# A decode step's attention: query projection with the row as weights, a first transfer in two, and one output block moved to the end

## The chip, the cores and the metric

The kernel runs on one core of a Trainium2 chip. The metric is the time of one execution on the device in microseconds (us). The program is told in terms of the core's engines: PE (TensorE, the matmuls, with its weight loads as PEld), DVE (VectorE), ACT (ScalarE), POOL (GpSimd) and SP (SyncE, which here issues nearly all transfers). 16 DMA engines move data between HBM and the on-chip memory SBUF; PSUM is the memory that PE writes to. SBUF and PSUM have 128 lanes (partitions).

## The reference

Four sequences decode one token each. The row x (4 x 640) is normed, goes through an attention with 32 heads over a cache of 4096 keys and values per head, and beside it through a small gated MLP; both results are added to x.

```python
def _A_ref(x, k_cache, v_cache, wq, wo):        # x (4,1,640), caches (4,32,4096,128)
    q = (x @ wq).reshape(B, Sq, Hq, Dh).transpose(0, 2, 1, 3)
    scores = jnp.einsum('bhqd,bhkd->bhqk', q, k) * Dh ** (-0.5)
    p = _softmax(scores, axis=-1)
    o = jnp.einsum('bhqk,bhkd->bhqd', p, v)
    return o.transpose(0, 2, 1, 3).reshape(B, Sq, Hq * Dh) @ wo

def _B_ref(x, w_in, w_sp, b_sp, w_out):         # w_in (640,1728), w_out (864,640)
    z = _gelu(jnp.einsum('bsd,df->bsf', x, w_in))
    z1, z2 = z[..., :Fh], _layernorm(z[..., Fh:], axis=-1)
    g = jnp.einsum('ts,bsf->btf', w_sp, z2) + b_sp[None, :, None]
    return jnp.einsum('bsf,fd->bsd', z1 * g, w_out)

xn = _layernorm(x, axis=-1)
return x + _A_ref(xn, k_cache, v_cache, wq, wo) + _B_ref(xn, w_in, w_sp, b_sp, w_out)
```

Everything is bfloat16. The two caches are 134 MB each, wq and wo 5.2 MB each; together with the MLP's weights some 282 MB are read once.

## The kernel before

**Tiles.** A tile is four heads of one sequence: 4 heads x 4096 keys x 128 values, 4 MB, laid out so that each of the 128 lanes holds 128 rows of the cache (32 KB in one piece). There are 32 K tiles and 32 V tiles, numbered i = 4 hg + b with the head group hg (0 to 7) and the sequence b (0 to 3).

**SBUF slots and the order of transfers.** Five slots of 4 MB (`KV_SLOTS`, pool `kv`) take turns. First the two parts of wq (4 MB and 1 MB, lines 90 to 93) and the MLP's weights sit in three of them, then K and V tiles in the order of the list `loads` (line 128). `pump` (line 140) issues the next load on SP when the slot's former occupant is in the set `used`. The last V tile comes in four pieces (`V_CUTS`: 64, 32, 16 and 16 of 128 columns). The output weights wo come in eight blocks of 640 KB, one a head group, into a pool of their own with one buffer (`wop`, line 69): block hg at tile i = 4 hg + 2 (line 698), the last block after the loop in four quarters (lines 155 to 157), so that it is the last thing in the queue. All these go through one hardware queue, SP's. Each transfer counts on one of eight completion semaphores in turn, so SP issues one only when the eighth before it has landed.

**The start.** x comes in on ACT's queue and is normed (lines 239 to 255); xn is turned into xnT, 128 lanes x 5 chunks x 4 sequences (lines 257 to 264). The query projection takes each of 160 blocks of wq (32 heads x 5 chunks, 128 x 128) as the matmul's weights and xnT's 4 columns as the moving part (lines 266 to 276), which gives q turned: 128 lanes x 32 heads x 4. `stage_q(i)` (line 421) makes the query of tile i ready for DVE: once a head group it transposes 16 rows back and copies them (`q_rows`), and for every tile it spreads them over 128 lanes with one matmul and one ACT copy (`qbc`). Then `gmlp` runs the MLP.

**A tile's work.** DVE multiplies K by the query in two halves (`product`, line 439) and folds 128 values to 64 (`fold_half`, line 448); PE sums them on with the identity (`sums`); DVE finishes the row sums and maxima; ACT takes the exponential; POOL lays the 128 probabilities of each lane out as matmul weights (line 517); PE multiplies them with V in four column groups of PSUM (`blocks`, line 526). After the fourth tile of a group, `group_den`, `group_norm`, `group_turn` and `group_pick` norm and turn the result, and `group_proj` (line 627) multiplies it by the wo block with 8 matmuls into the sum `out_ps`.

**The order** on PE, DVE, ACT and SP is written by hand in the loop from line 655 on, one tile behind another; POOL's is left to the scheduler. The end (lines 700 to 722): the last tiles' blocks, `pairs` for the last V pieces, `group_norm(7)`, `group_proj(7)`, two copies and two transfers out.

Of the kernel before, what the change touches and what calls it, by code (L numbers as in the profile page):

```python
# [9 lines left out]
FP32 = mybir.dt.float32  # L10
BF16 = mybir.dt.bfloat16
# [10 lines left out]
def kernel(  # L22
# [14 lines left out]
    nc = tc.nc  # L37
    P = nc.NUM_PARTITIONS
    Bsz, Sq, D = A_x.shape
    _, H, S, Dh = A_k_cache.shape  # L40
# [3 lines left out]
    DC = D // P  # L44
# [4 lines left out]
    HT = 4  # L49
    HG = H // HT  # L50
    NT = HG * Bsz
    LN = P // HT
    NC = HT * S // P
    HC = NC // 2
# [11 lines left out]
        edge = ctx.enter_context(tc.tile_pool(name="edge", bufs=1))  # L66
        edge.tile([P, skip], mybir.dt.uint8, name="edge")
    kv = ctx.enter_context(tc.tile_pool(name="kv", bufs=KV_SLOTS))
    wop = ctx.enter_context(tc.tile_pool(name="wop", bufs=1))
    const = ctx.enter_context(tc.tile_pool(name="const", bufs=1))  # L70
    work = ctx.enter_context(tc.tile_pool(name="work", bufs=1))
    small = ctx.enter_context(tc.tile_pool(name="small", bufs=2))
# [3 lines left out]
    ps_m = ctx.enter_context(tc.tile_pool(name="ps_m", bufs=2, space=PSUM))  # L76
# [11 lines left out]
    wq_v = A_wq.rearrange("(p c) n -> p c n", c=DC)  # L88
    wq_parts = []
    for c0, c1 in ((0, HT), (HT, DC)):  # L90
        t = slot("wq")[:, 0 : (c1 - c0) * HD].rearrange("p (c n) -> p c n", n=HD)
        nc.sync.dma_start(out=t, in_=wq_v[:, c0:c1, :])  # L92
        wq_parts += [(t, i) for i in range(c1 - c0)]

    wsp_bf = const.tile([1, 1], BF16)
# [9 lines left out]
        out=w_out_sb[:, 0:NFF, :], in_=B_w_out[0 : NFF * P].rearrange("(p k) n -> p k n", k=NFF)  # L105
# [47 lines left out]
    def load_wo(j):  # L153
        wo_tiles[j] = wop.tile([P, HT, D], BF16, name="wo")
        if j == HG - 1:
            for hh in range(HT):
                nc.sync.dma_start(out=wo_tiles[j][:, hh, :], in_=wo_h[j][:, hh, :])
            return
        nc.sync.dma_start(out=wo_tiles[j][:].rearrange("p r n -> p (r n)"), in_=wo_r[j])
# [5 lines left out]
    ident = const.tile([P, P], BF16)  # L165
# [9 lines left out]
    lane_diag = const.tile([P, LN], FP32)  # L175
    nc.vector.tensor_reduce(
        out=lane_diag[:],
        in_=ident_f[:].rearrange("p (h l) -> p l h", h=HT),
# [3 lines left out]
    for hh in range(HT):  # L182
        ps = slice(hh * LN, (hh + 1) * LN)
# [5 lines left out]
    CG = P // LN  # L189
# [3 lines left out]
    for e in range(2):  # L193
        nc.vector.tensor_reduce(
            out=sel[:, :, :, e],
            in_=ident_f[:].rearrange("p (g e k h) -> p e k h g", g=CG, e=2, k=GC)[:, e],
# [6 lines left out]
    for hh in range(HT):  # L203
# [3 lines left out]
        out=spread[:],  # L207
# [6 lines left out]
    q_lanes = const.tile([HT * Bsz, Bsz, P], BF16)  # L214
    nc.vector.tensor_copy(
        out=q_lanes[:].rearrange("r b (h l) -> r b h l", h=HT),
        in_=ident[: HT * Bsz, : HT * Bsz]
        .rearrange("r (h b) -> r b h", b=Bsz)[:, :, :, None]
        .to_broadcast([HT * Bsz, Bsz, HT, LN]),
    )  # L220

    hmask_bf = const.tile([P, HT], BF16)
    nc.vector.tensor_copy(out=hmask_bf[:], in_=hmask[:])

# [34 lines left out]
    for c in range(DC):  # L259
        nc.tensor.transpose(  # L260
            out=xnT_ps[:, c, :], in_=xn_v[:, c, :], identity=ident[:Bsz, :Bsz]
        )
    xnT = const.tile([P, DC, Bsz], BF16)
    nc.vector.tensor_copy(out=xnT[:], in_=xnT_ps[:])

    q_ps = ps_m.tile([P, H, Bsz], FP32, tag="m", name="q_ps")
    for h in range(H):
        for c in range(DC):
            t, i = wq_parts[c]
            nc.tensor.matmul(  # L270
                out=q_ps[:, h, :],
                lhsT=t[:, i, h * Dh : (h + 1) * Dh],
                rhs=xnT[:, c, :],
                start=(c == 0),
                stop=(c == DC - 1),
            )
    qT = const.tile([P, H, Bsz], BF16)
    nc.vector.tensor_copy(out=qT[:], in_=q_ps[:])  # L278

# [26 lines left out]
    def gmlp():  # L308
        zz, gw, gt, gz, sq = (gm[n] for n in ("zz", "gw", "gt", "gz", "sq"))
        zT = ps_pv.tile([P, 2, NFC, Bsz], FP32, tag="pv", name="zT")  # L310
        for t in range(2):
            f1 = t * Fh + NFF * P
            w_t = w_in_sb[:, :, t * Fh : f1].rearrange("p c (f k) -> p c k f", k=NFF)
            for k in range(NFC):
                for c in range(DC):
                    nc.tensor.matmul(
                        out=zT[: P if k < NFF else FT, t, k, :],
                        lhsT=w_t[:, c, k, :] if k < NFF else w_in_sb[:, c, f1 : f1 + FT],
                        rhs=xnT[:, c, :],
                        start=(c == 0),  # L320
                        stop=(c == DC - 1),
                    )
# [93 lines left out]
    qbcs, scores, pvs, blocks_sb = {}, {}, {}, {}  # L416
    sums_ps, maxes = {}, {}

    q_rows = {}

    def stage_q(i):
        hg, b = divmod(i, Bsz)
        if b == 0:
            qr_ps = ps_m.tile([HT * Bsz, Dh], BF16, tag="m", name="qr_ps")
            nc.tensor.transpose(
                out=qr_ps[:],
                in_=qT[:, HT * hg : HT * (hg + 1), :].rearrange("p h b -> p (h b)"),
                identity=ident[:],
            )
            q_rows[hg] = small.tile([HT * Bsz, Dh], BF16, name="q_rows")  # L430
            nc.scalar.copy(out=q_rows[hg][:], in_=qr_ps[:])  # L431
        qb_ps = ps_m.tile([P, Dh], FP32, tag="m", name="qbc_ps")
        nc.tensor.matmul(  # L433
            out=qb_ps[:], lhsT=q_lanes[:, b, :], rhs=q_rows[hg][:], start=True, stop=True
        )
        qbcs[i] = small.tile([P, Dh], BF16, name="qbc", bufs=3)
        nc.scalar.copy(out=qbcs[i][:], in_=qb_ps[:])  # L437

    def product(i, half):
        t = k_tiles[i][:, half * HC : (half + 1) * HC, :]  # L440
        nc.vector.tensor_tensor(  # L441
            out=t,
            in0=t,
            in1=qbcs[i][:, None, :].to_broadcast([P, HC, Dh]),
            op=ALU.mult,
        )

# [141 lines left out]
    def group_norm(hg):  # L589
        o_n = small.tile([P, HT, Bsz], BF16, name="o_n")  # L590
        nc.vector.tensor_tensor(
            out=o_n[:], in0=pvs.pop(hg)[:], in1=gr[hg][:], op=ALU.mult
        )
        gr[hg] = o_n
# [32 lines left out]
    def group_proj(hg):  # L627
        o_n = gr.pop(hg)
        for hh in range(HT):
            for half in range(2):  # L630
                nc.tensor.matmul(  # L631
                    out=out_sum(half),
                    lhsT=o_n[:, hh, :],
                    rhs=wo_tiles[hg][:, hh, half * NOH : (half + 1) * NOH],
                    start=False,
                    stop=(hg == HG - 1 and hh == HT - 1),
                )

    def group(i, fn):
        if 0 <= i < NT and i % Bsz == Bsz - 1:  # L640
            fn(i // Bsz)
# [13 lines left out]
    E = mybir.EngineType  # L655
    with tc.manual_schedule(engines={E.PE, E.DVE, E.Activation, E.SP}):
        stage_q(0)
        stage_q(1)
        gmlp()
        used.update(occupants[:3])  # L660
        pump()
        for i in range(NT):
            j = turns.get(i)
            product(i, 0)
            at(i - 1, row_sums, 1)
            at(i - 1, lane_max)
            at(i - 1, lay_max)
            at(i - 1, spread_max)
            group(turns.get(i - 1, -1), group_pick)
            group(turns.get(i - 1, -1), group_proj)  # L670
            fold_half(i, 0)
            at(i - 1, head_max)
            at(i - 1, exps)
            sums(i, 0)
            product(i, 1)
            if i + 2 < NT:
                stage_q(i + 2)
            due = [] if j is None else [j]
            if i == NT - 1:
                due += range(j + 1, NT - 2)  # L680
            for n, jj in enumerate(due):
                if n:
                    gather(due[n - 1])
                blocks(jj)
                group(jj, group_den)
                used.add(("v", jj))
            row_sums(i, 0)
            fold_half(i, 1)
            if due:
                gather(due[-1])  # L690
            for jj in due:
                group(jj, group_norm)
            sums(i, 1)
            for jj in due:
                group(jj, group_turn)
            used.add(("k", i))
            pump()
            if i % Bsz == 2 and i // Bsz < HG - 1:
                load_wo(i // Bsz)
        load_wo(HG - 1)  # L700
        row_sums(NT - 1, 1)
        lane_max(NT - 1)
        lay_max(NT - 1)
        spread_max(NT - 1)
        head_max(NT - 1)
        exps(NT - 1)
        blocks(NT - 2)
        group_den(HG - 1)
        blocks(NT - 1, 0, V_CUTS[1])
        gather(NT - 1, stop=False)  # L710
        for c0, c1 in zip(V_CUTS[1:], V_CUTS[2:]):
            pairs(NT - 1, c0, c1)
        group_norm(HG - 1)
        group_proj(HG - 1)

        res = work.tile([P, NOH], BF16, name="res")
        out_v = out.flatten_outer_dims()
        r0, r1 = slice(0, Bsz), slice(OG, OG + Bsz)
        nc.scalar.copy(out=res[r0], in_=out_ps[r0])
        nc.vector.tensor_copy(out=res[r1], in_=out_ps[r1])  # L720
        nc.scalar.dma_start(out=out_v[:, 0:NOH], in_=res[r0])
        nc.sync.dma_start(out=out_v[:, NOH:D], in_=res[r1])
# [30 lines left out]
```

## Time and profile before

| what | us |
|---|---|
| median of three runs | 664.45 (663.98 to 664.61) |
| the profiled execution | 664.67 |
| its span, first to last instruction | 662.8 |
| DVE busy | 492.9 (74%) |
| PE busy, of 2205 matmuls | 344.5 (52%) |
| POOL busy | 150.2 (23%) |
| ACT busy | 52.5 (8%) |
| DMA, mean over the span | 426 GB/s |

The span is what the profile draws; the execution's own time is 1.87 us longer. A profile is one execution, with all its accidents, and the runs without a profile scatter by 0.6 us. In the profile's groups a line number is that of the kernel; "idle before" is the time for which the engine stood still ahead of such an instruction. In the chain of waits each step is what released the step behind it.

### The profile page before, as it was taken

Reading aid. Unit: us, or ns where it says so; the run is one execution under the profiler, and the core shown is the slowest. Engines: PE = TensorE matmul, PEld = TensorE weight load, DVE = VectorE, ACT = ScalarE, POOL = GpSimd, SP = SyncE. Lnnn points to the kernel's source line nnn. Section 1 sums busy time; section 2 is a strip of 40 time slices with the busy share of each in tenths; the row PEclk is TensorE's granted clock in tenths of the full one; section 3 lists DMA queues with packets and bytes.
Section 4 is the critical chain, followed back from the end, with each engine's and each line's share of the span. In section 5 each row is a group of like instructions: output and inputs, shape, how many; then the busy total and the mean of one; then the engine's idle time right before and its main releaser. Section 6 shows DMA issues by size and latency. Waiting matters only on the chain.

```text
span 662.8 us, 5338 instructions
## 1 busy us (share of the span) xinstructions
PE 344.5 (52%) x2205; PEld 144.1 (22%) x2205; DVE 492.9 (74%) x334; ACT 52.5 (8%) x161; POOL 150.2 (23%) x51
## 2 busy tenths in 40 slices
PE   0636553636646545653437644474654655434576
PEld 0512221212222121221212212131211212212133
DVE  3289797867789677788767698767787899776960
ACT  0201100000010000100000001000100000000010
POOL 2002222112222112222112222112222132222220
PEclk9998676777576677776776657758666767678676
DMA  8999999999999999999999999999999999999996
GB/s 368 430 438 423 434 439 432 431 437 422 436 429 436 437 424 437 432 430 437 431 429 437 424 439 435 428 439 428 431 439 427 432 436 426 439 424 437 437 422 262
DMA packets 11972, 282.59 MB, mean 426 GB/s; under 512 B 1344, under 2 KB 1964, under 8 KB 3244
## 3 DMA queue, kind: packets, MB, share of 16 engines
q1 hardware_dynamic: 11928, 282.25, 99.0%
q8 instruction: 17, 0.28, 0.2%
q14 instruction: 7, 0.06, 0.0%
q10 hardware_dynamic: 20, 0.01, 0.0%
HBM read 282.24 MB, written 0.01 MB: 426 GB/s over the span
## 4 chain that ended last, share of the span: by engine, by line
issue 44%; DMA 29%; POOL 14%; DVE 9%; PE 3%; SPq 0%; ACT 0%; POOLq 0%; DVEq 0%; ACTq 0%
DMA k_nat<-in_A_k_cache_dram 21%; POOL pm L517 14%; DMA v_nat<-in_A_v_cache_dram 6%; DVE k_nat L441 5%; DVE k_nat L450 3%; PE s_ps L459 2%; DMA wo<-in_A_wo_dram 2%; PE pv_acc L532 1%; DVE s_sb L470 1%; DVE m L479 0%; PE pv L553 0%; POOL own_sum L577 0%; SPq L92 0%; SPq L104 0%; ACT pv_sb L542 0%
## 5 line engine op out<-in xcount | busy, mean ns | idle before, releaser
L441 DVE TENSOR_TENSOR k_nat<-k_nat,qbc 128x8192 bf16<-128x8192 bf16 x64 | 282.9, 4420 | 100.4 <-DMA k_nat<-in_A_k_cache_dram 100.2
L517 POOL TENSOR_TENSOR pm<-p,hmask_bf 128x512 bf16<-128x512 bf16 x32 | 142.4, 4452 | 496.2 <-ACT p L508 496.2
L459 PE MATMUL s_ps<-k_nat,ident 128*128 128x512 bf16 x512 | 188.9, 535 | 67.0 <-DVE k_nat L450 67.0
L450 DVE TENSOR_TENSOR k_nat<-k_nat 128x4096 bf16<-128x4096 bf16 x64 | 151.9, 2373 | 0.0
L492 PE MATMUL max_ps<-lay,head_scale 128*128 128x32 f32 x64 | 19.0, 388 | 176.3 <-ACT lay L485 176.3
L532 PE MATMUL pv_acc<-v_nat,pm 128*32 128x512 bf16 x1008 | 85.0, 498 | 39.0 <-POOL pm L517 35.6
L459 PEld LDWEIGHTS <-ident 128*128 128x128 bf16 x512 | 67.6, 134 | 168.6 <-issue 151.1
L492 PEld LDWEIGHTS max_ps<-lay,head_scale 128*128 128x128 f32 x64 | 14.8, 288 | 190.5 <-ACT lay L485 190.5
L532 PEld LDWEIGHTS <-pm 128*32 128x32 bf16 x1008 | 29.5, 117 | 82.4 <-POOL pm L517 42.1
L470 DVE TENSOR_REDUCE s_sb<-s_ps 128x64 f32<-128x512 f32 x64 | 43.4, 677 | 4.1 <-PE s_ps L459 4.1
L485 ACT ACTIVATE lay<-lane_diag,m 128x32 f32<-128x32 f32 x32 | 10.3, 321 | 340.2 <-DVE m L479 340.2
L586 DVE RECIPROCAL rden<-den 128x16 f32<-128x16 f32 x8 | 2.1, 258 | 30.5 <-PE den L584 30.5
L553 PE MATMUL pv<-sel,pv_sb 128*128 128x8 f32 x128 | 18.6, 272 | 9.3 <-ACT pv_sb L542 9.3
L553 PEld LDWEIGHTS pv<-sel,pv_sb 128*128 128x128 f32 x128 | 17.1, 208 | 15.8 <-ACT pv_sb L542 15.8
L508 ACT ACTIVATE p<-s_sb,nb 128x128 bf16<-128x128 f32 x32 | 12.8, 401 | 63.8 <-DVE nb L499 63.8
L437 ACT CAST qbc<-qbc_ps 128x128 bf16<-128x128 f32 x32 | 8.4, 267 | 85.1 <-PE qbc_ps L433 85.1
L542 ACT COPY pv_sb<-pv_acc 128x512 f32<-128x512 f32 x16 | 9.4, 586 | 65.6 <-PE pv_acc L532 65.6
L479 DVE TENSOR_REDUCE m<-s_sb 128x1 f32<-128x128 f32 x32 | 9.2, 286 | 1.1
L433 PE MATMUL qbc_ps<-q_rows,q_lanes 16*128 16x128 bf16 x32 | 8.2, 264 | 2.7 <-ACT q_rows L431 2.7
L278 DVE CAST qT<-q_ps 128x128 bf16<-128x128 f32 x1 | 0.3, 292 | 12.5 <-PE q_ps L270 12.5
L270 PE MATMUL q_ps<-xnT,wq 128*128 128x4 bf16 x160 | 4.6, 166 | 8.7 <-DMA wq<-in_A_wq_dram 8.7
L631 PE MATMUL out_ps<-wo,o_r 128*4 128x320 bf16 x56 | 8.0, 435 | 0.0
(90 smaller groups left out, 89.7 us busy)
## 6 DMA issues: line engine op xcount, KB each, us to landing
k_nat<-in_A_k_cache_dram SPq DMA_DIRECT2D x32, 4096.0 KB, 38.7
v_nat<-in_A_v_cache_dram SPq DMA_DIRECT2D x31, 4096.0 KB, 33.3
wo<-in_A_wo_dram SPq DMA_DIRECT2D x7, 640.0 KB, 40.5
wq<-in_A_wq_dram SPq DMA_DIRECT2D x1, 4096.0 KB, 12.7
w_sb<-in_B_w_in_dram SPq DMA_DIRECT2D x1, 2160.0 KB, 19.4
v_nat<-in_A_v_cache_dram SPq DMA_DIRECT2D x1, 2048.0 KB
wq<-in_A_wq_dram SPq DMA_DIRECT2D x1, 1024.0 KB, 14.7
v_nat<-in_A_v_cache_dram SPq DMA_DIRECT2D x1, 1024.0 KB
```

The source lines that it names most:

```text
L441: nc.vector.tensor_tensor(out=t, in0=t, in1=qbcs[i][:, None, :].to_broadcast([P, HC, Dh]), op=ALU.mult,)
L450: nc.vector.tensor_tensor(out=t[:, :, 0:HD2], in0=t[:, :, 0:HD2], in1=t[:, :, HD2:Dh], op=ALU.add)
L459: nc.tensor.matmul(out=s[:], lhsT=ident[:], rhs=t[:, :, g * RW : (g + 1) * RW], start=(g == 0), stop=(g == n - 1),)
L470: nc.vector.tensor_reduce(out=scores[i][:, half * HC : (half + 1) * HC], in_=sums_ps.pop((i, half))[:], axis=AX.X, op=ALU.add,)
L479: nc.vector.tensor_reduce(out=m1[:], in_=scores[i][:], axis=AX.X, op=ALU.max)
L485: nc.scalar.activation(out=d[:], in_=lane_diag[:], func=ACT.Copy, scale=maxes[i][:, 0:1])
L492: nc.tensor.matmul(out=ps[:], lhsT=head_scale[:], rhs=maxes[i][:], start=True, stop=True)
L508: nc.scalar.activation(out=p[:], in_=scores.pop(i)[:], func=ACT.Exp, bias=nb[:], scale=scale_qk, accum_out=acc[hg % NACC][:, b : b + 1],)
L517: nc.gpsimd.tensor_tensor(out=p_m[b][:, :, e : e + GC * HT].rearrange("p g (c h) -> p g c h", h=HT), in0=p[:].rearrange("p (g c) -> p g c" ...
L532: nc.tensor.matmul(out=pv_acc[g * LN : (g + 1) * LN, :], lhsT=pm[:, c // GC, :], rhs=v_nat[:, c : c + GC, :].rearrange("p c d -> p (c d)") ...
L542: nc.scalar.copy(out=pv_sb[:], in_=pv_acc[:])
L553: nc.tensor.matmul(out=pvs[hg][:, :, b - 1 : b + 1], lhsT=pv_sb[:, k * Dh : (k + 1) * Dh], rhs=sel[:, k, :, :], start=(k == 0), stop=stop ...
```

## The change

It has three parts.

1. **Query projection.** xnT is widened to 32 columns a chunk (4 used, the rest zeros) and becomes the weights; wq moves through with 512 columns at a time, eight head groups of four heads, in four column groups of each of two PSUM tiles: 40 matmuls, chunk by chunk. q then lies in rows: lane 32 g + b, head group g or g + 4. `stage_q(hg)` is now called once a head group, two tiles ahead: four matmuls with a placing matrix `place` (made by POOL) bring 16 rows together, an ACT copy, four spreading matmuls, one ACT copy of 512 columns.
2. **First transfer.** The first wq part (4 MB) is issued as 16 lanes and 112 lanes.
3. **Wo block 6.** The pool `wop` has two buffers; block 6 is loaded after the loop, ahead of block 7, and `group_proj(6)` runs at the end, ahead of `group_proj(7)`.

```diff
-    wop = ctx.enter_context(tc.tile_pool(name="wop", bufs=1))
+    wop = ctx.enter_context(tc.tile_pool(name="wop", bufs=2))
...
-        nc.sync.dma_start(out=t, in_=wq_v[:, c0:c1, :])
+        for p0, p1 in ((0, 16), (16, P)) if c0 == 0 else ((0, P),):
+            nc.sync.dma_start(out=t[p0:p1], in_=wq_v[p0:p1, c0:c1, :])
...
+    place = const.tile([P, HT, HT * Bsz], BF16)
+    nc.gpsimd.memset(place[:], 0.0)
+    for hh in range(HT):
+        nc.gpsimd.tensor_copy(
+            out=place[:, hh, hh * Bsz : (hh + 1) * Bsz], in_=lane_diag[:, 0:Bsz]
+        )
...
-    xnT = const.tile([P, DC, Bsz], BF16)
-    nc.vector.tensor_copy(out=xnT[:], in_=xnT_ps[:])
-    q_ps = ps_m.tile([P, H, Bsz], FP32, tag="m", name="q_ps")
-    for h in range(H):
-        for c in range(DC):
-            t, i = wq_parts[c]
+    xnT = const.tile([P, DC, LN], BF16)
+    nc.gpsimd.memset(xnT[:], 0.0)
+    nc.vector.tensor_copy(out=xnT[:, :, 0:Bsz], in_=xnT_ps[:])
+    q_sb = const.tile([P, HG // CG, HT * Dh], BF16)
+    q_ps = [
+        ps_m.tile([P, HT * Dh], FP32, tag="m", name="q_ps") for _ in range(HG // CG)
+    ]
+    for c in range(DC):
+        t, i = wq_parts[c]
+        for hg in range(HG):
+            g = hg % CG
             nc.tensor.matmul(
-                out=q_ps[:, h, :],
-                lhsT=t[:, i, h * Dh : (h + 1) * Dh],
-                rhs=xnT[:, c, :],
+                out=q_ps[hg // CG][g * LN : (g + 1) * LN, :],
+                lhsT=xnT[:, c, :],
+                rhs=t[:, i, hg * HT * Dh : (hg + 1) * HT * Dh],
                 start=(c == 0),
                 stop=(c == DC - 1),
             )
-    qT = const.tile([P, H, Bsz], BF16)
-    nc.vector.tensor_copy(out=qT[:], in_=q_ps[:])
+    nc.vector.tensor_copy(out=q_sb[:, 0, :], in_=q_ps[0][:])
+    nc.scalar.copy(out=q_sb[:, 1, :], in_=q_ps[1][:])
...
+    def stage_q(hg):
+        g, ps = hg % CG, slice(hg % CG * LN, (hg % CG + 1) * LN)
+        qr_ps = ps_m.tile([HT * Bsz, Dh], FP32, tag="m", name="qr_ps")
+        for hh in range(HT):
+            nc.tensor.matmul(
+                out=qr_ps[:],
+                lhsT=place[ps, hh, :],
+                rhs=q_sb[ps, hg // CG, hh * Dh : (hh + 1) * Dh],
+                start=(hh == 0),
+                stop=(hh == HT - 1),
+            )
+        q_rows = small.tile([HT * Bsz, Dh], BF16, name="q_rows")
+        nc.scalar.copy(out=q_rows[:], in_=qr_ps[:])
+        qb_ps = ps_m.tile([P, Bsz, Dh], FP32, tag="m", name="qbc_ps")
+        for b in range(Bsz):
+            nc.tensor.matmul(
+                out=qb_ps[:, b, :], lhsT=q_lanes[:, b, :], rhs=q_rows[:], start=True, stop=True
+            )
+        qbcs[hg] = small.tile([P, Bsz, Dh], BF16, name="qbc")
+        nc.scalar.copy(out=qbcs[hg][:], in_=qb_ps[:])
...
         stage_q(0)
-        stage_q(1)
         gmlp()
...
-            group(turns.get(i - 1, -1), group_proj)
+            if turns.get(i - 1, -1) // Bsz < HG - 2:
+                group(turns.get(i - 1, -1), group_proj)
...
-            if i + 2 < NT:
-                stage_q(i + 2)
+            if i % Bsz == 2 and i // Bsz + 1 < HG:
+                stage_q(i // Bsz + 1)
...
-            if i % Bsz == 2 and i // Bsz < HG - 1:
+            if i % Bsz == 2 and i // Bsz < HG - 2:
                 load_wo(i // Bsz)
+        load_wo(HG - 2)
         load_wo(HG - 1)
...
         group_norm(HG - 1)
+        group_proj(HG - 2)
         group_proj(HG - 1)
```

More of the change, by code (lines that the diff above doesn't have):

```diff
@@ L318, in gmlp @@
                         lhsT=w_t[:, c, k, :] if k < NFF else w_in_sb[:, c, f1 : f1 + FT],
-                        rhs=xnT[:, c, :],
+                        rhs=xnT[:, c, 0:Bsz],
                         start=(c == 0),
@@ L417 @@
     sums_ps, maxes = {}, {}
[L419 to L425, printed above, removed]
+    def stage_q(hg):
[3 more added lines that the diff above has]
+            nc.tensor.matmul(
                 out=qr_ps[:],
-                in_=qT[:, HT * hg : HT * (hg + 1), :].rearrange("p h b -> p (h b)"),
-                identity=ident[:],
-            )
[L430 to L437, printed above, removed]
+                lhsT=place[ps, hh, :],
+                rhs=q_sb[ps, hg // CG, hh * Dh : (hh + 1) * Dh],
+                start=(hh == 0),
+                stop=(hh == HT - 1),
+            )
+        q_rows = small.tile([HT * Bsz, Dh], BF16, name="q_rows")
[7 more added lines that the diff above has]
+        nc.scalar.copy(out=qbcs[hg][:], in_=qb_ps[:])
     def product(i, half):
@@ L443, in product @@
             in0=t,
-            in1=qbcs[i][:, None, :].to_broadcast([P, HC, Dh]),
+            in1=qbcs[i // Bsz][:, i % Bsz, None, :].to_broadcast([P, HC, Dh]),
             op=ALU.mult,
```

## The prediction, made before the changed kernel was run

> **What bounds the kernel now.** I read the page's slices first, then the chain that ended last, then two stretches in 1 to 6 us windows (start and end), then the trace's DMA packet records.
>
> ```profile
> span 662.8 us, 5338 instructions
> GB/s 368 430 438 423 434 439 432 431 437 422 436 429 436 437 424 437 432 430 437 431 429 437 424 439 435 428 439 428 431 439 427 432 436 426 439 424 437 437 422 262
> q1 hardware_dynamic: 11928, 282.25, 99.0%
> q8 instruction: 17, 0.28, 0.2%
> ```
>
> The 16 DMA engines move 282 MB at some 434 GB/s in every slice but the first (368) and the last (262). DVE, the busiest engine, is at 74%, and waits 100 us for K. So the change, which moves the same bytes, can be worth something only where the queue starts, where it ends, and where something takes time from a DMA engine. In between, each transfer lands at least 28 us after its issue and takes 9.7 us itself, so its issue may come 18 us later at no cost.
>
> The start (columns: stretch, busy us of PE, PEld, DVE, ACT and POOL, PE clock, DMA share, GB/s):
>
> ```profile
> 0.00:2.00 2.00, 0.00 (x0) 0.00 (x0) 0.92 (x11) 0.10 (x1) 1.44 (x7) 1.00 0.57 150
> 2.00:3.00 1.00, 0.00 (x0) 0.00 (x0) 0.89 (x6) 1.00 (x1) 1.00 (x3) 1.00 0.66 229
> 3.00:4.00 1.00, 0.00 (x0) 0.00 (x0) 1.00 (x3) 0.18 (x1) 1.00 (x3) 1.00 1.00 426
> 4.00:6.00 2.00, 0.00 (x0) 0.00 (x0) 1.56 (x6) 0.29 (x1) 0.91 (x2) 1.00 0.72 311
> 6.00:12.00 6.00, 0.71 (x7) 0.35 (x7) 1.75 (x8) 0.00 (x0) 0.00 (x0) 1.00 1.01 437
> ```
>
> Full rate comes only after some 4 us. The packet records say why. A lane of the first wq transfer is one packet of 32 KB. The 16 engines' first packets begin between 1.76 and 2.92 us and most take 1.6 to 2.4 us; all later ones take 1.21. The two that begin late, at 2.76 and 2.92, take 1.21 at once. So the early ones seem to stand waiting until about 2.45. The second packets begin between 3.66 and 4.61 us, 3.90 in the mean.
>
> The end, by the chain and by PE's timeline:
>
> ```profile
> 606.26 40.90 DMA v_nat<-in_A_v_cache_dram
> 647.16 0.02 issue
> 647.17 12.45 DMA wo<-in_A_wo_dram
> 659.62 0.04 issue
> 659.66 0.47 PE out_ps L631 x2
> ```
>
> ```profile
> 655.60 2.01 PE L565 MATMUL pv<-pm,v_nat 128*128 128x4 bf16 x64
> 657.87 0.96 PE L631 MATMUL out_ps<-wo,o_n 128*4 128x320 bf16 x6 [0.27 <-DVE o_n L591]
> 659.66 0.43 PE L631 MATMUL out_ps<-wo,o_n 128*4 128x320 bf16 x2 [0.82 <-DMA wo<-in_A_wo_dram]
> ```
>
> PE has only the last two output matmuls left and waits 0.82 us for the last wo quarter. Again the packets say more:
>
> ```profile
> 655.00:656.00 1.00, 1.00 (x20) 1.00 (x20) 0.00 (x0) 0.00 (x0) 0.00 (x0) 0.50 0.79 311
> 656.00:657.00 1.00, 1.00 (x39) 0.93 (x35) 0.00 (x0) 0.00 (x0) 0.00 (x0) 0.50 0.58 218
> 657.00:658.00 1.00, 0.73 (x19) 0.60 (x20) 0.18 (x1) 0.00 (x0) 0.00 (x0) 0.50 0.56 198
> 658.00:659.00 1.00, 0.84 (x6) 0.33 (x3) 0.00 (x0) 0.00 (x0) 0.00 (x0) 0.50 0.04 14
> ```
>
> Seven engines are done by 656.2, nine by 657.6 to 658.32: a transfer lands with its slowest engine. The quarter's last data packet ends at 658.32, but its last completion write comes at 658.58, because a 16 KB packet of instruction code (queue q8) holds that engine from 657.63 to 658.59; it counts as landed at 659.62. Earlier pieces land 0.33 us after their last packet (V31's last: 656.64, landed 656.97). Without the code packet the quarter would be there at 658.32 + 0.33 = 658.65, 0.97 us sooner.
>
> **The change part by part.** The sum goes against the profiled execution: 664.67 us, 1.87 outside the span; it is 0.22 over the median 664.45.
>
> *Query projection.* Out: 160 matmuls with 4 columns (15.90 to 20.22 us) and 8 transposes; in: 40 with 512 columns in four column groups and 32 placing ones. The row of that form is pv_acc, 16 in 1.05 us at clock 1.0, 66 ns each: 32 of them (2.1 us) fit between the landings of the two wq parts (13.45, 15.86), eight follow, so q is ready at about 16.5 instead of 20.3. Bound from above: at the 498 ns that one takes alone, 20 us, to 33.5. Neither ends anything: DVE's first product waits for K0, landed at 34.77. Value 0. What stands before it: POOL's memset of xnT now comes behind four copies that need lane_diag (6.91); with 2 us of pm memsets it is done near 10.5, 3 us before wq lands. V0's issue goes from 20.23 to about 16.5, with K0 and K1 still queued to 44.4. The staging per group (8 matmuls, a copy of 512 columns at 0.59 us by the pv_sb row, once in four tiles) replaces four of 0.28 + 0.27; PE and ACT are idle half the time or more, and DVE wants the result two tiles later. 0.
>
> *What this does to code.* 96 fewer matmuls, each with its weight load: PE's 4410 recorded become 4218. The 17 code packets of 16 KB come one per some 256 PE instructions: 4410/256 = 17.2, 4218/256 = 16.5. Matched by count, the seventeenth is asked for at about recorded instruction 4250 of 4426 (the others' packets follow such a point by 3 to 8 us); PE then has 4234. So it should fall away or come behind the last matmul. The sixteenth moves from 635 to about 651 us; it takes its 0.9 us from an engine either way.
>
> *Wo block 6 last.* It leaves the middle of the queue (packets at 584 us) for the place behind V31. Same bytes: the queue's end stays. V29 to V31 land 640 KB / 434 GB/s = 1.5 us earlier, so the pairs are done near 656. Wo 6 ends where V31 ended, landed 656.97. Behind it stand now 16 matmuls, eight pairs at 0.267 us (starts 657.87, 658.10, 658.36): the last pair starts at 656.97 + 7 x 0.267 = 658.84, after the last quarter's 658.65, and ends at 659.31 instead of 660.13: **-0.82**. PE becomes the bound there, for 0.2 us. Bounds: 0 if a code packet falls there again, -1.0 if PE runs at clock 1.0 (it has 0.5). SP: in both kernels every issue waits for the transfer eight before it; the last quarter so waits for V31's first piece (652.05, less 1.5) instead of V30; 3.2 MB, 7 us of work, is queued then. 0.
>
> *Sixteen lanes first.* One packet per engine, then seven. If the stagger and the slow first packets come from descriptors being made for 128 lanes, all engines run from about 1.76, and second packets begin at 1.76 + 1.21 = 2.97 instead of 3.90: -0.93 in the mean, -0.69 to -1.64 by engine. What counts is the engine that ends last. If the first packets are slow because memory is, 0. I take **-0.9**, since the late starters at full speed speak for the first. The extra issue (0.41 us on SP) shifts later issues, which have cover: eight packets an engine last to 13 us.
>
> [...]
>
> Sum: 664.67 - 0.82 - 0.9 = **662.95**.
>
> **Rivals.** *Tail only*: first packets are slow whoever asks. For it: nine start within 0.2 us and still take 1.7 to 2.4. 664.67 - 0.82 = 663.85. *Start only*: the code packet stays at the end, or the sixteenth comes late enough to hit one of the slow engines there. For it: the request point is known to some 20 instructions, and one delay reaches 15 us. 664.67 - 0.9 = 663.77. *Neither*: 664.6. *Slower*: the 16 lanes do not go one to an engine. At eight lanes an engine, two engines get 8 + 7 packets instead of 8 and end 7 x 1.21 = 8.5 us late, 671.5 with the tail's gain; at four, 3 x 1.21 = 3.6, 667.5. It decides from two extra packets on one engine. Against it: the four lanes of x begin 16 ns apart, each 53 ns long, so on different engines.
>
> **How the numbers follow.** Forecast 0.55, tail only 0.16, start only 0.13, neither 0.04, slower 0.12. Faster by over 0.2% (about what a measurement of this kernel can tell from no change) is below 663.12: four fifths of the forecast (start of 0.73 or more) and a little of the next two, 0.50; slower 0.12; within, 0.38. Both parts at their bounds give 664.67 - 1.64 - 1.0 = 662.0, none 664.6; the range 661.9 to 664.5 leaves out the slower case and some of "neither". The forecast's own range is 662.2 to 663.6.
>
> **What would show it.** Start: second packets near 3 us, the 2 to 3 us window near 400 GB/s, K0 landing near 33.9. Code: 16 packets on q8, none in the last 3 us. Tail: last wo landing 0.33 us behind its last packet, no wait of PE between the last pairs, the last pair ending near 658.4. Wrong if K0 lands at 34.7, if a code packet sits beside the last wo, or if a few engines run on alone at the end.

## The result and the profile after

| | before | changed |
|---|---|---|
| median us, four runs each on one chip | 664.22 (663.89 to 664.61) | 672.98 (672.80 to 673.08) |
| ratio, with its 95% interval | | 1.0131 (1.0114 to 1.0149) |
| span of the profiled execution | 662.8 | 671.2 |

The forecast was 662.95, faster. The kernel is 8.8 us slower. The page of the changed kernel, the lines that answer to those of before:

```profile
span 671.2 us, 5117 instructions
GB/s 215 356 433 435 433 428 427 439 435 432 432 430 437 435 427 432 432 436 434 425 435 429 435 434 431 432 435 432 434 431 432 435 435 434 427 430 434 435 425 278
q1 hardware_dynamic: 11944, 282.25, 99.1%
q8 instruction: 16, 0.26, 0.1%
```

The bytes are the same, every slice from the third on runs at the old rate, and the queue of code (q8) has the 16 packets that were forecast. The loss is in the first two slices, 33.6 us in which the queue moved 215 and 356 GB/s instead of 368 and 430. The same stretches as before, with one more (columns: stretch, length, busy us of PE, PEld, DVE, ACT, POOL, PE clock, DMA share, GB/s):

```profile
0.00:2.00 2.00, 0.00 (x0) 0.00 (x0) 0.92 (x11) 0.11 (x1) 1.44 (x8) 1.00 1.33 199
2.00:3.00 1.00, 0.00 (x0) 0.00 (x0) 0.89 (x4) 1.00 (x1) 1.00 (x2) 1.00 0.95 131
3.00:4.00 1.00, 0.00 (x0) 0.00 (x0) 0.56 (x3) 0.17 (x1) 0.12 (x1) 1.00 0.00 0
4.00:6.00 2.00, 0.27 (x5) 0.27 (x5) 1.57 (x7) 0.29 (x1) 0.00 (x0) 1.00 1.12 197
6.00:12.00 6.00, 0.44 (x5) 0.08 (x2) 1.25 (x6) 0.00 (x0) 2.85 (x8) 1.00 0.79 197
12.00:20.00 8.00, 0.00 (x0) 0.00 (x0) 0.00 (x0) 0.00 (x0) 0.00 (x0) 1.00 1.04 262
```

From 4 to 20 us the DMA engines are busy (shares of 0.79 to 1.12), yet move 197 to 262 GB/s where the kernel before moved 437 from 6 to 12 us. (A packet's time and bytes are booked where it begins, hence the 0.00 and the shares above 1.) Busy at half the rate means packets that take twice as long: in the records the 16 packets of the first transfer, 32 KB each as before, take 3.2 to 3.8 us, and those of the 112 lanes 2.4 to 3.4 the first on each engine and mostly 1.8 to 2.3 the six behind it, with a median of 2.22 for the 112 against 1.21 before. The first 4 MB end at 21.73 us instead of 13.10, 8.6 us late. The chain of waits shows that nothing behind it makes this good:

```profile
0.74 7.11 DMA wq<-in_A_wq_dram
7.84 0.02 issue
7.86 35.54 DMA k_nat<-in_A_k_cache_dram
43.40 0.02 issue
43.42 4.44 DVE k_nat L458
```

The transfer of K0 lands at 43.40 us; it was 34.77, by the same step of the chain in the kernel before:

```profile
3.60 31.16 DMA k_nat<-in_A_k_cache_dram
```

The 8.6 us of the start reach the end whole, since the queue has no slack from there on (425 to 439 GB/s in every slice but the first two and the last). At the end of PE's timeline stands the other half of the change (columns: start, us, engine, line, operation, count, idle time before with its releaser):

```profile
659.86 1.90 PE L549 MATMUL pv_acc<-v_nat,pm 128*32 128x512 bf16 x16 [1.40 <-DMA v_nat<-in_A_v_cache_dram]
662.49 1.88 PE L570 MATMUL pv<-sel,pv_sb 128*128 128x8 f32 x8 [0.74 <-ACT pv_sb L559]
664.22 1.85 PE L582 MATMUL pv<-pm,v_nat 128*128 128x4 bf16 x64
666.11 1.23 PE L648 MATMUL out_ps<-wo,o_r 128*4 128x320 bf16 x8
667.13 1.28 PE L648 MATMUL out_ps<-wo,o_n 128*4 128x320 bf16 x8
```

All 16 output matmuls stand in a row with no wait between the pairs, as forecast. Two things come together ahead of them: PE ends the `pairs` at 666.07, at the end of its own chain from V31's first piece on (659.86), and wo block 6 lands at 666.07.

### The profile page after: what moved, and what is told of

Its sections match the earlier page's. It is cut to its first block, busy times and chain, and to the rows that moved or that the text cites. A ratio compares the mean times of both kernels' runs of the same rounds, so it can differ in the third digit from the quotient of the medians.

```text
span 671.2 us, 5117 instructions
## 1 busy us (share of the span) xinstructions
PE 349.4 (52%) x2109; PEld 143.6 (21%) x2109; DVE 492.2 (73%) x334; ACT 49.3 (7%) x138; POOL 151.3 (23%) x57
## 4 chain that ended last, share of the span: by engine, by line
issue 48%; DMA 26%; POOL 15%; DVE 7%; PE 3%; SPq 0%; ACT 0%; POOLq 0%; DVEq 0%; ACTq 0%
DMA k_nat<-in_A_k_cache_dram 21%; POOL pm L534 15%; DMA wo<-in_A_wo_dram 4%; DVE k_nat L458 4%; DVE k_nat L467 2%; PE s_ps L476 2%; DMA wq<-in_A_wq_dram 1%; PE pv_acc L549 1%; DVE s_sb L487 0%; SPq L124 0%; PE out_ps L648 0%; PE pv L570 0%; POOL own_sum L594 0%; DVE m L496 0%; ACT pv_sb L559 0%
## 5 line engine op out<-in xcount | busy, mean ns | idle before, releaser
L476 PE MATMUL s_ps<-k_nat,ident 128*128 128x512 bf16 x512 | 193.4, 546 | 68.4 <-DVE k_nat L467 68.4
L549 PE MATMUL pv_acc<-v_nat,pm 128*32 128x512 bf16 x1008 | 87.5, 508 | 39.8 <-POOL pm L534 35.7
L502 ACT ACTIVATE lay<-lane_diag,m 128x32 f32<-128x32 f32 x32 | 10.3, 321 | 398.0 <-DVE m L496 398.0
L286 PE MATMUL q_ps<-wq,xnT 128*32 128x512 bf16 x40 | 4.5, 631 | 16.3 <-DMA wq<-in_A_wq_dram 16.3
L516 DVE TENSOR_REDUCE nb<-max_ps 128x1 f32<-128x32 f32 x32 | 5.8, 183 | 0.9 <-PE max_ps L509 0.9
```

Of the source, the lines that this page charges most:

```text
L476: nc.tensor.matmul(out=s[:], lhsT=ident[:], rhs=t[:, :, g * RW : (g + 1) * RW], start=(g == 0), stop=(g == n - 1),)
L502: nc.scalar.activation(out=d[:], in_=lane_diag[:], func=ACT.Copy, scale=maxes[i][:, 0:1])
L549: nc.tensor.matmul(out=pv_acc[g * LN : (g + 1) * LN, :], lhsT=pm[:, c // GC, :], rhs=v_nat[:, c : c + GC, :].rearrange("p c d -> p (c d)") ...
```

## The experiments

All times were taken beside runs of the kernel before on the same chip; a ratio is to those runs. Where a diff names `c0 == 0`, it is the first wq part, 4 MB, of which every lane takes one packet of 32 KB.

My theory after the result was that the split alone costs the time, through the set of lanes that a transfer writes. Its rivals: the order or number of transfers, the rows of HBM, the new projection or the new tail.

**The change without its split.**

```diff
-        for p0, p1 in ((0, 16), (16, P)) if c0 == 0 else ((0, P),):
-            nc.sync.dma_start(out=t[p0:p1], in_=wq_v[p0:p1, c0:c1, :])
+        nc.sync.dma_start(out=t, in_=wq_v[:, c0:c1, :])
```

> The changed kernel with the first wq part in one transfer of 128 lanes again. Theory S (the split costs the 9 us, the other two parts are worth about -0.8): 663.9 us, full rate from 4 us on, K0 landing near 34.7. Theory Q (the cost is in the query projection or in the moved wo block, and the slow start only goes with them): about 672, with first packets of 2 us and more as in the changed kernel.

Measured: 663.76 (663.53 to 665.02, ten runs) against 664.53, ratio 0.9992 (0.9983 to 1.0002). So the split costs 672.98 - 663.76 = 9.2 us (from two sets of runs, in which the kernel before differs by 0.3 us: 664.22 and 664.53), and the two other parts together bring little or nothing that can be told. K0 lands near 34.5 us again, the sum of start and length here:

```profile
3.81 30.72 DMA k_nat<-in_A_k_cache_dram
```

In the profile the two other parts do what was forecast. PE's tail:

```profile
656.91 1.23 PE L647 MATMUL out_ps<-wo,o_r 128*4 128x320 bf16 x8 [0.95 <-DMA wo<-in_A_wo_dram]
657.93 1.28 PE L647 MATMUL out_ps<-wo,o_n 128*4 128x320 bf16 x8
```

PE waits for wo block 6, landed at 656.87 (forecast 656.97), and ends with the last pair at 659.25 by the records (forecast 659.31; before 660.13). The last code packet is at 649.16, none at the end.

**The kernel before with the split and nothing else.**

```diff
-        nc.sync.dma_start(out=t, in_=wq_v[:, c0:c1, :])
+        for p0, p1 in ((0, 16), (16, P)) if c0 == 0 else ((0, P),):
+            nc.sync.dma_start(out=t[p0:p1], in_=wq_v[p0:p1, c0:c1, :])
```

> The kernel before with only the first wq part split into 16 and 112 lanes. Theory S: 664.2 + 9.3 = 673.5 us, packets of the first part 1.9 to 3.6 us long instead of 1.21. Theory Q: 664.

Measured: 673.49 (673.06 to 673.80), ratio 1.0137 (1.0122 to 1.0152), 9.0 us. Packets 2.13 us, the first part done at 21.94. The split is enough by itself.

**The same issue count, split by columns**: all 128 lanes, first one chunk (8 KB a lane), then three.

```diff
-        for p0, p1 in ((0, 16), (16, P)) if c0 == 0 else ((0, P),):
-            nc.sync.dma_start(out=t[p0:p1], in_=wq_v[p0:p1, c0:c1, :])
+        for d0, d1 in ((0, 1), (1, 4)) if c0 == 0 else ((0, 1),):
+            nc.sync.dma_start(out=t[:, d0:d1, :], in_=wq_v[:, c0 + d0 : c0 + d1, :])
```

> The changed kernel with the first wq part split another way: 128 lanes of one of its four chunks (8 KB a lane), then 128 lanes of three chunks (24 KB). If what costs is that fewer than 128 lanes are written at a time, there is no loss: 663.9 us, or up to 0.9 less if a short first transfer helps the start as I had predicted. If a split costs by itself, whatever its shape: about 672.

Measured: 663.66 (663.53 to 664.08), ratio 0.9988 (0.9979 to 0.9998). A second transfer by itself costs nothing. The run also bears on the slow first packets. Its start:

```profile
0.00:2.00 2.00, 0.00 (x0) 0.00 (x0) 0.92 (x11) 0.12 (x1) 1.44 (x8) 1.00 0.42 55
2.00:3.00 1.00, 0.00 (x0) 0.00 (x0) 0.89 (x6) 1.00 (x1) 1.00 (x2) 1.00 0.43 141
3.00:4.00 1.00, 0.00 (x0) 0.00 (x0) 0.60 (x5) 0.46 (x2) 0.13 (x1) 1.00 1.01 426
```

The first packets are a quarter as large, begin from 1.75 us on, and all but one of the first sixteen still end only between 2.6 and 3.4, where later ones of that size take 0.31 us. By that, an estimate, the bytes begin to flow near 2.5 us for packets of 8 KB as for those of 32 KB (ends of 3.7 to 4.6 in the kernel before, less 1.21). Fewer lanes do not bring them sooner: with 32 lanes first (every fourth, below; later packets take 1.22 us) the first packets begin at 2.09 to 2.92 and end at 3.8 to 5.1 us, with the 128 lanes of the kernel before at 3.7 to 4.6. The 16 first packets of the changed kernel, one on each engine, begin at 1.75 to 1.96 (twelve) and 2.56 to 2.68 (four) and end at 5.0 to 6.5; when their bytes begin to flow, the records do not show.

**64 and 64 lanes.**

```diff
-        for p0, p1 in ((0, 16), (16, P)) if c0 == 0 else ((0, P),):
+        for p0, p1 in ((0, 64), (64, P)) if c0 == 0 else ((0, P),):
```

> The changed kernel with the split at 64 and 64 lanes. [...] Theory R (the rows that are read together from HBM are at fault): 64 rows are nearly as many as 128, 664 to 666.

Measured: 674.40 (674.26 to 674.64), ratio 1.0152 (1.0136 to 1.0167); packets 2.57 us, the part done at 22.86. It is not the small first transfer that hurts. The stretch from 12 to 36 us:

```profile
12.00:36.00 24.00, 8.96 (x118) 5.88 (x118) 1.47 (x6) 2.71 (x4) 0.00 (x0) 0.92 1.01 327
```

**Lanes or rows: eight transfers of 16 lanes, two by two.** The lanes of a transfer lie together or apart (every eighth), and so do its rows of wq in HBM. The two mixed kernels put rows of wq into lanes that do not match those of x, so that q and all that follows come from permuted weights; the work stays the same. One run each, beside one of the kernel before at 664.29.

```diff
-            nc.sync.dma_start(out=t[p0:p1], in_=wq_v[p0:p1, c0:c1, :])
+            for g in range(8):   # c0 == 0; the four kernels:
+                nc.sync.dma_start(out=t[16 * g : 16 * (g + 1)], in_=wq_v[16 * g : 16 * (g + 1), c0:c1, :])
+                nc.sync.dma_start(out=t[g::8], in_=wq_v[16 * g : 16 * (g + 1), c0:c1, :])
+                nc.sync.dma_start(out=t[16 * g : 16 * (g + 1)], in_=wq_v[g::8, c0:c1, :])
+                nc.sync.dma_start(out=t[g::8], in_=wq_v[g::8, c0:c1, :])
```

> First wq part as eight transfers of 16 lanes, lanes 16g to 16g+15, from the 16 neighbouring rows of wq. [...]

> The same eight transfers, but written to every eighth lane (g, g+8, ...), from 16 neighbouring rows; the lanes no longer match x's, so q is computed from permuted weights and the output isn't the reference's. [...] Theory R: rows as before, so the same time as with lanes together.

> Eight transfers to 16 neighbouring lanes from every eighth row (output not the reference's, for the same reason). [...] Theory R: as fast as lanes apart, rows apart.

> Eight transfers to every eighth lane from every eighth row. [...] Theory R: faster than both runs with rows together.

| | rows together | rows apart |
|---|---|---|
| lanes together | 689.19 us, packets 4.46 us | 689.75, 4.48 |
| lanes apart | 673.68, packets 2.53 us | 674.52, 2.54 |

Going across changes nothing in the packets, going down nearly halves them: the lanes in SBUF decide, not the rows in HBM. The stretch from 12 to 36 us with lanes and rows together, and then with the lanes apart:

```profile
12.00:36.00 24.00, 0.00 (x0) 0.00 (x0) 0.00 (x0) 0.00 (x0) 0.00 (x0) 1.00 0.94 109
```

```profile
12.00:36.00 24.00, 8.90 (x118) 5.82 (x118) 1.62 (x7) 3.01 (x6) 0.00 (x0) 0.90 0.98 323
```

In the first the 16 engines are busy for 24 us (share 0.94) and move 109 GB/s, while no compute engine has anything to do.

**Every fourth lane (four transfers) and every second lane (two).**

```diff
+            for g in range(4):
+                nc.sync.dma_start(out=t[g::4], in_=wq_v[g::4, c0:c1, :])
...
+            for g in range(2):
+                nc.sync.dma_start(out=t[g::2], in_=wq_v[g::2, c0:c1, :])
```

> The changed kernel with the first wq part as four transfers of 32 lanes, every fourth lane each, two lanes an engine. [...]

> The first wq part as two transfers of 64 lanes, every second lane each. If an even spread over the lanes is enough, 1.21 us a packet and 663.9, against 674.4 with 64 adjacent lanes. If a part of 64 lanes is slow whichever: 674.

Measured, one run each: 664.14 beside 664.30, and 663.87 beside 664.54; packets 1.22 and 1.21 us, the full rate. The stretch from 2 to 10 us, which lies within the first wq part, first with 64 neighbouring lanes and then with every second lane:

```profile
2.00:10.00 8.00, 0.71 (x7) 0.35 (x7) 3.47 (x16) 1.49 (x2) 3.98 (x10) 1.00 1.15 238
```

```profile
2.00:10.00 8.00, 0.71 (x7) 0.35 (x7) 3.53 (x16) 1.58 (x2) 3.98 (x10) 1.00 1.00 393
```

So half the lanes at a time, every second one, were written at the full rate: 393 GB/s (401 in the kernel before), where 64 neighbours gave 238, and the part is done at 13.18 us (13.10 with one transfer), where 64 neighbours held it until 22.86.

**112 and 16 lanes; 32 and 96 lanes.** By then it was open whether the 112 lanes were slow only because 16 had gone ahead.

```diff
-        for p0, p1 in ((0, 16), (16, P)) if c0 == 0 else ((0, P),):
+        for p0, p1 in ((0, 112), (112, P)) if c0 == 0 else ((0, P),):
...
+        for p0, p1 in ((0, 32), (32, P)) if c0 == 0 else ((0, P),):
```

> The changed kernel with 112 lanes (0 to 111) first and 16 lanes (112 to 127) behind. If the 16 lanes ahead only leave the engines in each other's way: 112 lanes at 1.21 us a packet, about 666. If a transfer of 112 adjacent lanes is slow by itself: packets of about 2 us from the first on, about 673 as in the changed kernel.

> The changed kernel split at 32 and 96 lanes. [...] If a part of adjacent lanes is slow unless it is the whole 128: +9.7, 673.5.

Measured, one run each beside 664.54: 672.88 and 673.36. With the 112 lanes first their packets take 1.8 to 2.25 us (medians of sixteen at a time) from the start, and the 16 lanes behind them 3.0 to 4.15; with 32 and 96 lanes they take 2.2 to 2.57 throughout. With packets of 32 KB, 112 and 96 neighbouring lanes were slow by themselves. With small ones it was otherwise: the kernel before has one transfer to 96 neighbouring lanes, the rest of `w_out` (line 107) with 1280 bytes a lane, and its packets take 0.055 us in the median, as do those of wo's last quarters, 1280 bytes to each of 128 lanes. What makes the difference, the size or what the other engines do at that time, no run here tells.

**The tail's two parts, each alone.** First wo block 6 last in the kernel before, then the changed kernel without split and with the wo block in its old place.

```diff
+    wop = ctx.enter_context(tc.tile_pool(name="wop", bufs=2))
...
+            if turns.get(i - 1, -1) // Bsz < HG - 2:
+                group(turns.get(i - 1, -1), group_proj)
...
-            if i % Bsz == 2 and i // Bsz < HG - 1:
+            if i % Bsz == 2 and i // Bsz < HG - 2:
...
+        load_wo(HG - 2)
...
+        group_proj(HG - 2)
```

> The kernel before with only wo block 6 loaded and used last. Theory C (the gain of the changed kernel's tail is the code packet that falls away, which the smaller projection brings): still 17 code packets, one of them in the last 6 us, the last wo quarter again late behind it, 664.3 us, as before. Theory W (the gain comes from the block's new place): 663.7.

> The kernel before with only the query projection changed (one transfer of 128 lanes, wo block 6 in its old place). Theory C: 16 code packets, none in the last 3 us, the last wo quarter lands 0.33 us behind its last data packet, PE ends near 659.1 in the span: 663.6 us. Theory W: 664.4.

Measured: 664.53 (664.34 to 665.42), ratio 1.0004 (0.9995 to 1.0013), and 664.19 (663.35 to 665.54), ratio 0.9998 (0.9989 to 1.0007): neither brings anything alone. The two tails of PE, first with the wo block alone:

```profile
656.95 1.23 PE L631 MATMUL out_ps<-wo,o_r 128*4 128x320 bf16 x8 [0.95 <-DMA wo<-in_A_wo_dram]
658.44 1.55 PE L631 MATMUL out_ps<-wo,o_n 128*4 128x320 bf16 x8 [0.26 <-DMA wo<-in_A_wo_dram]
```

```profile
652.01 1.90 PE L548 MATMUL pv_acc<-v_nat,pm 128*32 128x512 bf16 x16 [0.76 <-DMA v_nat<-in_A_v_cache_dram]
...
658.49 1.23 PE L647 MATMUL out_ps<-wo,o_n 128*4 128x320 bf16 x8 [0.27 <-DVE o_n L607]
```

With the wo block alone there are still 17 code packets, the last at 656.37 for 0.94 us, and PE waits for block 7 before its last eight matmuls: the last quarter lands at 659.51, against 658.53 in the kernel with one transfer, which has the same tail and no code packet there. With the projection alone there are 16, and the last quarter lands at 658.53 instead of 659.62, as theory C says. But PE comes to it late: it does the 16 `pv_acc` matmuls in 1.90 us (1.05 in the kernel before, with a granted clock of 1.00; 1.90 in the changed kernel too, with 0.50), is itself the bound, and ends at 659.76. The sixteenth code packet, at 650.75, stands beside V31's first piece and does not make it late: it lands at 652.0, as in the kernel before (652.05).

**Wo block 6 between V31's pieces** (without the split), to take the 0.95 us wait of PE out of the tail.

```diff
+            if c1 == V_CUTS[2] and len(cuts) > 2:
+                load_wo(HG - 2)
...
-        load_wo(HG - 2)
         load_wo(HG - 1)
...
+            if c1 == V_CUTS[2]:
+                group_proj(HG - 2)
         group_norm(HG - 1)
-        group_proj(HG - 2)
```

> The changed kernel with one first transfer, and wo block 6 loaded between the second and third piece of the last V tile and used between their matmuls. Theory: with one transfer PE waits 0.95 us for block 6 and is then the bound with 16 matmuls in a row (2.34 us); here eight of them fall into that wait, so that only the last quarter's landing is left: PE ends near 659.0 instead of 659.25, 663.5 us. If PE is not the bound there: 663.8, as with the block behind V.

Measured: 663.87, ratio 0.9992 (0.9983 to 1.0001), no better than with both blocks behind V31. V31's last piece, now behind block 6 in the queue, lands at 656.93, about when PE is through with block 6's matmuls (657.01), so that the last eight matmuls start at 658.22 behind DVE's o_n.

## Why the prediction was wrong

**Sixteen lanes first** is the step that failed: taken at -0.9, measured at +9.2 (changed kernel against the one without the split) and +9.0 (split alone). It failed twice.

- The gain was not there. It stood on the guess that the first packets wait for the descriptors of 128 lanes. With 32 lanes first the first packets ended no sooner (3.8 to 5.1 us against 3.7 to 4.6), and with packets of 8 KB the first bytes, by the estimate above, still came near 2.5 us. The rival "tail only" ("first packets are slow whoever asks") was right on this, and I had its evidence on the page: nine engines that begin within 0.2 us and all take long. I also left out a third late starter, at 2.84, whose packet took 1.77 us: the late ones did not all run at full speed.
- The loss was not among my terms. I priced a lane at 1.21 us, the row of packets of a 128-lane transfer, and carried that row to transfers of other shapes. The same 32 KB take 1.21 us with 128 lanes, every second or every fourth, 2.1 to 2.6 with 112, 96, 64 or 32 neighbours or with every eighth lane, and 4.46 with 16 neighbours. An engine's eight packets add up to 18.8 us in the changed kernel (in the mean of the engines 3.5, then 2.8, then six of 1.9 to 2.3) and to 10.3 in the kernel before: +8.5, about what the landing of K0 shows (+8.6).

The slower rival came near in its price (8.5 us), by luck, since it was wrong in its mechanism. (Its sum should read 672.3, 663.85 + 8.5; 671.5 counts the start's gain as well.) It had several lanes queue on one engine; in the records all 16 first packets are under way (the last from 2.68 us on) before one ends (at 4.96), so, by that, each has an engine of its own. Had I bounded the 112-lane packets by rows of the trace, I would have found none of a transfer with fewer lanes and as many bytes: the one to 96 lanes has packets of 1280 bytes, and they are not slow. Then an open bound belonged in the range, and "slower" a larger chance than 0.12.

As rates, 16 packets of 32 KB in 4.46 us (16 neighbours), 2.57 (64 neighbours), 2.53 (every eighth lane) and 1.21 (every second lane) are 118, 204, 207 and 433 GB/s, and in 2.22 us (the 112 neighbours) 236. The number of lanes does not order them: 64 lanes ran at 204 as neighbours and at 433 as every second lane, and 112 neighbours at little more than the 16 of every eighth lane. By what mechanism the lanes set the rate, no run shows. That it matters which lane each engine writes at one time is only a guess: the packet records name no lane. This stays open, as does whether a stored lane or the engine's path to it is the slow part.

**Wo block 6 last** and **What this does to code** were right in the profile. Forecast -0.82, seen -0.88 (660.13 to 659.25) without the split; the seventeenth code packet is gone and PE is the bound. From the start of one code packet to the next, PE's recorded instructions go on by 254 in the mean in the kernel before (158 to 396) and by 251 in the changed one (211 to 311) (the forecast took 256). In time that kernel measured 663.76 where "tail only" said 663.85, though its interval (0.9983 to 1.0002) does not exclude no gain. Two things were not said: that each part alone gives nothing, since the one leaves the code packet and the other, in its profiled execution, meets a PE that takes 1.90 us for the 16 `pv_acc` matmuls instead of 1.05; and that the gain hangs on PE's speed there and on where a code packet falls, two accidents of some 1 us each. Why PE was slow there is open. In the changed kernel itself some 0.3 of the 0.88 is left: 668.47 - 660.13 is 8.3 against the 8.6 of the start. Its wo block 6 lands at 666.07, 9.2 us behind that of the kernel without the split, 0.6 us more than the 8.6 by which the first 4 MB end late. A code packet at 657.80 (0.93 us) stands beside V31's first piece, which lands 0.97 us behind its last data packet (0.36 in the kernel before); that this is the 0.6 us is not shown.

**Query projection** at 0 was right. Without the split q is in rows from 18.1 us and spread by 19.8 (I had put q at 16.5), while K0 lands near 34.5; it was never on the path.

**The signs I named.** "Wrong if K0 lands at 34.7" was the right place to look, though I named only one side of it. The 2 to 3 us stretch should have reached 400 GB/s and had 131.

The best of these kernels is the change split by columns, 663.66, at 0.9988 of before (0.9979 to 0.9998); with one transfer it is 663.76. Both differ from the kernel before by less than I called tellable.

## What to carry to other kernels

Here, in a kernel bound by its transfers, 8.6 us lost at the head of the queue made the time 8.8 us longer, so price a changed shape of transfer by a row of that shape, and if the trace has none, say that the bound is open. Cutting the first 4 MB (packets of 32 KB, or of 8 and 24 KB by columns) cost nothing by columns (663.66 us) or by every second or fourth lane (663.87 and 664.14), 8.3 to 25.5 us in blocks of neighbouring lanes and 9.4 to 10.2 by every eighth lane; where a transfer with packets of this size is to be cut, try the first ways. When work is moved at the end of a kernel, look where the code packets fall before and after, in the packet records: one beside wo's last quarter went with a landing some 1 us later here (659.62 against 658.53).

## What the runs showed of the hardware that I had not expected

- A 32 KB packet to one lane is not one price: 1.21 us to 4.46 us by the lanes that its transfer writes, with the 16 engines busy (DMA shares of 0.94 from 12 to 36 us with 16 neighbours, 1.15 and 1.00 from 2 to 10 us with 64 neighbours and every second lane). The rows in HBM made no difference (4.46 and 4.48, 2.53 and 2.54). Packets of 1280 bytes took 0.055 us with 96 neighbouring lanes as with 128.
- The first bytes of the queue came, by estimate, near 2.5 us, about 0.75 us after the first packets began, for packets of 8 KB and of 32 KB (by the ends of the first packets, less the 0.31 and 1.21 us that later ones take).
- A 16 KB packet of code took 0.88 to 1.09 us in the kernel before and 0.88 to 1.05 in the changed one. With one beside the last transfers wo's last quarter landed at 659.62 and 659.51 (kernel before, wo block alone), without at 658.53 (one transfer, projection alone). Beside V31's first piece it did not make that land late in these last two.
- The same 16 `pv_acc` matmuls of the tail took 1.05 us in some kernels and 1.90 in others, with the clock that PE had there: 1.05 with 1.00 granted over these us in the kernel before, 1.90 with 0.50 in the changed kernel.
